# Half of the last block's weights, split into their two parts where they are converted and stored from SyncE

## The chip, the core and the metric

The kernel runs on one core of one Trainium2 chip. The metric is the device time of one execution in microseconds, as the median of three runs; lower is better. A difference under about 0.2%, some 4 us here, can hardly be told from no change.

## The reference

Three layers follow one another, for 2304 tokens of 512 features: a linear attention, a mixture of eight experts in which every token passes through every expert, and a dense block with the activation h - tanh(h). Cut to what matters:

```python
attn = linear_attention(q, k, v, omega)          # 4 x 8 heads x 576 x 64
x = attn.transpose(0, 2, 1, 3).reshape(2304, 512)
P = balanced_softmax(x @ w_gate)                 # 2304 x 8
out = 0
for e in range(8):                               # w1: 8 x 512 x 1024, w2: 8 x 1024 x 512
    out += P[:, e:e + 1] * (maximum(x @ w1[e], 0) @ w2[e])
h = out @ w_in                                   # w_in: 512 x 2048, drawn as doubles
return (h - tanh(h)) @ w_out                     # w_out: 2048 x 512, doubles
```

The weights of the last block are 64-bit numbers in DRAM; everything else is float32.

## The kernel before

Every matrix product is made of three products of rounded parts: a float32 operand is held as a high part, rounded for TensorE, and a low part, the rest. `split` (L107, L110) makes them: ScalarE casts the high part, and GpSimd or VectorE subtracts it from the source. A tile `u` (128 x 2 x 256) holds the two parts of one piece of a first-layer weight, a tile `v` (128 x 2 x 512) those of a second-layer weight; 16 tiles u and 8 tiles v stand in rings.

The tokens are cut into three superblocks of 768. The experts are done for all three, one superblock after another, and then the last block for all three. In the second and third superblock the products of the experts are made by a scheme with seven products for eight; their weights' parts come back from DRAM copies (`u<-st` at L290, `y<-st` at L312), which SyncE loads, in the order of the program, into rings of 16 and 12 pieces. A step of an expert's loop is a "quad", of which a superblock has 32.

The last block goes through its 2048 hidden features in four groups of 512, g = 0 to 3, for each superblock. For a group it needs eight tiles u and four tiles v. The generator `weights()` makes them: jobs of kind "i" load 512 KB of the float32 copy `win32` into a tile `rqi` and split four tiles u from it, with the subtraction on GpSimd; jobs of kind "s" load 256 KB of `wout32` into a tile `rs` and split one tile v, two of a group's four on GpSimd and two on VectorE. This is done again for every superblock, as the two parts don't stay in SBUF. In `shrink` the product `p` (L1481) is turned into h - tanh(h) by ScalarE and VectorE, its high part is cast by ScalarE (L1509), and its low part is made by GpSimd (L1510); `l` (L1521) is the product with `v`.

The float32 copies are made by `convert`, since no engine reads doubles: VectorE takes a piece of 128 x 256 doubles `r` apart in six instructions, with one of ScalarE and one of GpSimd between, and SyncE stores the float32 piece `x` (L1179). There are 64 pieces, 16 for each group. It runs in the background, a step at a time: 27 pieces in the first superblock, where a step follows every third tick, and 37 in the third, where a piece takes eight steps. There a piece's tile `r` is one of a ring of three (tag "rs"), and the load of piece k+3 (L1150) is issued right behind the store of piece k.

All loads and stores named here stand in SyncE's one queue, in the program's order; an entry that waits holds up those behind it. Each also waits for the one issued eight places before it.

Of the kernel before, what the change touches and what calls it, by code (L numbers as in the profile page):

```python
# [10 lines left out]
F32 = mybir.dt.float32  # L11
# [9 lines left out]
def performer_moe_kernel(ctx, tc, q, k, v, omega, wg, w1, w2, win64, wout64, out):  # L21
    nc = tc.nc
# [60 lines left out]


    CW = 256
    cjobs, made, converted = [], {}, [0]

    def to_convert(src, dst, r, c):
        cjobs.append((src[r : r + P, c : c + CW], dst[r : r + P, c : c + CW]))

    for g in range(NGM):
        for f in range(g * GF, (g + 1) * GF, 2):
            for r in range(0, DM, P):
                to_convert(win64, win32, r, f * P)
            made["i", f] = len(cjobs)
        for f in range(g * GF, (g + 1) * GF):
            for c in range(0, DM, CW):
                to_convert(wout64, wout32, f * P, c)
            made["o", f] = len(cjobs)
    NCV = len(cjobs)  # L100

    u1, u2, uw = {}, {}, {}
    spent1, spent2, spentx, spentw = set(), set(), set(), set()
# [80 lines left out]
    def weights():  # L184
# [2 lines left out]
        jobs = []  # L187
        for Q in range(NQ):
            e, q = divmod(Q, NQE)
            jobs.append(("q", Q, lambda e=e, q=q: load_quad(e, q), 0))  # L190
            for f in (2 * q, 2 * q + 1):
                jobs.append(("s", 2 * Q + f % 2, lambda e=e, f=f: load_slab(w2[e][f * P : (f + 1) * P, :]), 0))
        for g in range(NG + 1):
            jobs.append(("c", g, None, 0))
        for s in range(NSB):
            for g in range(NGM):
                for f in range(g * GF, (g + 1) * GF, 2):
                    jobs.append(("i", 0, lambda f=f: load_win(f), NCV if s else made["i", f]))
                for f in range(g * GF, (g + 1) * GF):
                    jobs.append(  # L200
                        (
                            "s",
                            -1,
                            lambda f=f: load_slab(wout32[f * P : (f + 1) * P, :]),
                            NCV if s else made["o", f],
                        )
                    )
        ahead = []

        def slabs(Q):  # L210
# [3 lines left out]
        def fetch():  # L214
            while jobs and len(ahead) < 5:
                k = jobs[0][0]
                if jobs[0][3] > converted[0]:
                    break
                if k == "c":
                    if ahead:  # L220
                        break
                elif sum((x[0] == "s") == (k == "s") for x in ahead) >= (3 if k == "s" else 2):
                    break
                elif k != "s" and not rqfree():
                    break
                k, a, f, _ = jobs.pop(0)
                ahead.append((k, a, f and f()))
# [18 lines left out]
        while ahead or jobs:  # L246
# [75 lines left out]
            elif k == "i":  # L322
                raw, done = raw
                for i in range(4):
                    while not free1(n1):
                        yield 1
                    o = i // 2 * P
                    unit1(n1, raw[:, i % 2 * 2 : i % 2 * 2 + 2, o : o + P], nc.gpsimd)
                    n1 += 1
                    yield None  # L330
                done[0] = True
            else:
                while not free2(n2):
                    yield 1
                k = (n2 - N2) % NV - NU2 if n2 >= N2 else -1
                if k < 0:
                    u = vtile([P, 2, 512], f"v{n2}", lambda n=n2: n in spent2)
                elif k == 0:
# [7 lines left out]
                if a >= 0:  # L346
# [793 lines left out]
    def convert(raws, work, fine):  # L1140
        V = nc.vector
        bits = lambda w: struct.unpack("f", struct.pack("I", w))[0]
        big, small = bits(0x47EFFFFF), bits(0x38100000)

        def ld():
            if not cjobs or halt[0]:
                return None
            src, dst = cjobs.pop(0)
            r = raws(f"r64_{len(cjobs)}")
            nc.sync.dma_start(r, src.bitcast(U32).rearrange("p (n t) -> p n t", t=2))  # L1150
            return r, dst

        nx = [ld(), ld()] if fine else [ld()]
        for _ in range(16 if fine else 1):
            yield
        while nx[0]:
            r, dst = nx.pop(0)
# [8 lines left out]
            yield  # L1166
            V.scalar_tensor_tensor(h, c, 0xC0000000, t, ALU.bitwise_and, ALU.bitwise_or)
            if fine:
                yield
            V.tensor_scalar(t, h, 0xFF800000, None, ALU.bitwise_and)  # L1170
            yield
            V.scalar_tensor_tensor(xf, lo, 2.0**-52, t.bitcast(F32), ALU.mult, ALU.mult)
            yield
            nc.scalar.activation(cf, cf, AF.Abs)
            nc.gpsimd.tensor_tensor(xf, xf, h.bitcast(F32), ALU.add)
            yield
            yield
            V.scalar_tensor_tensor(xf, cf, small, xf, ALU.is_ge, ALU.mult)
            nc.sync.dma_start(dst, xf)  # L1179
            converted[0] += 1  # L1180
            yield


# [457 lines left out]
    for st in stages:  # L1641
# [47 lines left out]
        elif kind == 0:  # L1689
            for Q in range(NQ):  # L1690
                e, g = Q // NQE, (s - 1) * NQ + Q
                if s == 1 and Q == 0:
                    set_banks("ppn", 4, 4)
                    kept.extend(lbank("l2") for _ in range(2))
                if s == 1 and Q == 1:
                    first_turn()
                if s == 2 and Q == 1:
                    halt[0] = False
                    pace[4] = 26
# [112 lines left out]
```

## Time and profile before

| | before |
|---|---|
| median of three runs | 2061.15 us (2060.12 to 2062.38) |
| the profiled execution's own time | 2059.81 us |
| its span, first to last instruction | 2058.0 us |
| TensorE (PE) busy | 2011.1 us, 98% of the span |
| VectorE (DVE) busy | 1562.3 us, 76% |
| ScalarE (ACT) busy | 1420.8 us, 69% |
| GpSimd (POOL) busy | 1471.3 us, 71% |

The profiled execution lies 1.34 us under the median of the runs. PE's busy time is that of pipelined matmuls; what counts is where it is idle, and what ended that idle time.

### The profile page before, as it was taken

Reading aid. Unit: us, or ns where it says so; the run is one execution under the profiler, and the core shown is the slowest. Engines: PE = TensorE matmul, PEld = TensorE weight load, DVE = VectorE, ACT = ScalarE, POOL = GpSimd, SP = SyncE. Lnnn points to the kernel's source line nnn. Section 1 sums busy time; section 2 is a strip of 40 time slices with the busy share of each in tenths; the row PEclk is TensorE's granted clock in tenths of the full one; section 3 lists DMA queues with packets and bytes.
Section 4 is the critical chain, followed back from the end, with each engine's and each line's share of the span. In section 5 each row is a group of like instructions: output and inputs, shape, how many; then the busy total and the mean of one; then the engine's idle time right before and its main releaser. Section 6 shows DMA issues by size and latency. Waiting matters only on the chain.

```text
span 2058.0 us, 37571 instructions
## 1 busy us (share of the span) xinstructions
PE 2011.1 (98%) x11408; PEld 1878.2 (91%) x11408; DVE 1562.3 (76%) x3004; ACT 1420.8 (69%) x3498; POOL 1471.3 (71%) x1855
## 2 busy tenths in 40 slices
PE   8999999999999999999999999999999989999999
PEld 7776888898999899999999999999999878989998
DVE  8885768889886665666666667777775589999997
ACT  7885333443442577777777688788788878888885
POOL 7885877887784588888888767676676675565652
PEclk9999999999999999999999999999999999999999
DMA  6545977798786688999988988988878532131310
GB/s 172 136 140 176 367 273 272 274 334 278 274 277 238 198 279 308 346 329 332 332 311 307 346 284 294 336 287 287 300 271 300 179 116 77 62 127 43 113 47 31
DMA packets 348056, 486.45 MB, mean 236 GB/s; under 512 B 71616, under 2 KB 166736, under 8 KB 347856
## 3 DMA queue, kind: packets, MB, share of 16 engines
q1 hardware_dynamic: 341712, 476.66, 67.6%
q10 hardware_dynamic: 6144, 7.40, 1.1%
q8 instruction: 92, 1.51, 0.3%
q14 instruction: 108, 0.88, 0.1%
HBM read 339.17 MB, written 144.78 MB: 235 GB/s over the span
## 4 chain that ended last, share of the span: by engine, by line
PE 79%; DVE 6%; POOL 6%; ACT 3%; issue 3%; DMA 2%; SPq 0%; ACTq 0%; DVEq 0%; POOLq 0%
PE l L1521 21%; PE Y L1380 18%; PE b L1205 13%; PE e L1205 9%; PE a L1205 8%; PE p L1481 7%; PE X L1380 2%; POOL tmp L616 2%; POOL eq L776 1%; POOL h L1289 1%; DMA y<-st 1%; DVE t L1502 0%; POOL u L110 0%; DVE t L1503 0%; DVE x L110 0%
## 5 line engine op out<-in xcount | busy, mean ns | idle before, releaser
L1380 PE MATMUL Y<-h,y 128*128 128x384 f32 x2394 | 486.3, 336 | 9.5 <-ACT Y L1372 9.0
L1521 PE MATMUL l<-v,h 128*128 128x512 f32 x2016 | 483.6, 393 | 8.9 <-POOL h L1510 3.8
L1521 PEld LDWEIGHTS l<-v,h 128*128 128x128 f32 x2016 | 375.5, 188 | 87.5 <-POOL h L1510 4.7
L1380 PEld LDWEIGHTS Y<-h,y 128*128 128x128 f32 x2394 | 419.9, 188 | 15.4 <-ACT Y L1372 14.5
L1289 POOL TENSOR_TENSOR h<-t,h 128x384 fp32r<-128x384 f32 x223 | 229.9, 1031 | 175.7 <-ACT h L1286 147.6
L1205 PE MATMUL b<-x,u 128*128 128x384 f32 x1728 | 348.5, 336 | 2.2 <-DVE t L1299 1.7
L1396 ACT COPY seven<-Y 128x384 f32<-128x384 f32 x534 | 247.1, 482 | 134.9 <-PE Y L1380 131.7
L1205 PEld LDWEIGHTS b<-x,u 128*128 128x128 f32 x1728 | 304.9, 188 | 8.0 <-DVE t L1299 2.0
L1372 ACT COPY Y<-seven 128x384 f32<-128x384 f32 x558 | 263.0, 488 | 3.8 <-DVE seven L1394 3.8
L1289 POOL TENSOR_TENSOR h<-h,h 128x384 fp32r<-128x384 f32 x192 | 203.6, 1066 | 43.3 <-ACT h L1286 40.1
L1205 PE MATMUL a<-x,u 128*128 128x384 f32 x1152 | 231.6, 335 | 1.6 <-POOL u L110 1.3
L1205 PE MATMUL e<-x,u 128*128 128x384 f32 x1152 | 231.2, 335 | 0.0
L1481 PE MATMUL p<-x,u 128*128 128x384 f32 x1152 | 210.6, 338 | 1.9 <-DVE seven L1394 1.9
L1481 PEld LDWEIGHTS p<-x,u 128*128 128x128 f32 x1152 | 203.8, 189 | 5.8 <-DVE seven L1394 2.2
L1205 PEld LDWEIGHTS a<-x,u 128*128 128x128 f32 x1152 | 202.3, 188 | 3.3 <-POOL u L110 1.7
L1205 PEld LDWEIGHTS e<-x,u 128*128 128x128 f32 x1152 | 202.5, 188 | 0.0
L110 POOL TENSOR_TENSOR v<-rs,v 128x256 fp32r<-128x256 f32 x176 | 144.0, 846 | 63.3 <-ACT v L107 54.9
L1510 POOL TENSOR_TENSOR h<-t,h 128x384 fp32r<-128x384 f32 x94 | 96.3, 1025 | 122.5 <-ACT h L1509 117.7
L1286 ACT CAST h<-t 128x384 fp32r<-128x384 f32 x224 | 115.7, 518 | 35.4 <-POOL t L1342 17.8
L1304 DVE TENSOR_TENSOR t<-b,t 128x384 f32<-128x384 f32 x64 | 35.6, 556 | 123.1 <-PE b L1205 123.1
L1556 DVE SCALAR_TENSOR_TENSOR acc<-l,pt,acc 128x512 f32<-128x512 f32 x144 | 104.7, 744 | 27.6 <-PE l L1521 25.9
L107 ACT CAST u<-s 128x256 fp32r<-128x256 f32 x128 | 49.4, 409 | 105.8 <-POOL u L110 42.0
(346 smaller groups left out, 3817.0 us busy)
## 6 DMA issues: line engine op xcount, KB each, us to landing
u<-st SPq DMA_DIRECT2D x448, 256.0 KB, 5.2
y<-st SPq DMA_DIRECT2D x336, 256.0 KB, 5.0
st<-u SPq DMA_DIRECT2D x224, 256.0 KB, 3.9
rs<-in_moe_w_dram SPq DMA_DIRECT2D x128, 256.0 KB, 4.8
st<-y SPq DMA_DIRECT2D x128, 256.0 KB, 5.7
st<-v SPq DMA_DIRECT2D x96, 256.0 KB, 5.2
rq<-in_moe_w_dram SPq DMA_DIRECT2D x32, 512.0 KB, 4.7
rqi<-win SPq DMA_DIRECT2D x24, 512.0 KB, 4.8
```

Source lines behind the costliest of these rows:

```text
L107: nc.scalar.copy(dst[:, 0], src)
L110: eng.tensor_tensor(dst[:, 1, i : i + w], src[:, i : i + w], dst[:, 0, i : i + w].bitcast(F32), ALU.subtract)
L1205: nc.tensor.matmul(ps[:, :TB], u[:, wi, c], x[:, xi, c], start=(start and m == 0), stop=(stop and m == 5), skip_group_check=True,)
L1286: nc.scalar.copy(H[k][:, 0], src)
L1289: eng.tensor_tensor(H[k][:, 1], src, H[k][:, 0].bitcast(F32), ALU.subtract)
L1372: nc.scalar.copy(cell[0], xacc[i][:, d])
L1380: nc.tensor.matmul(ps, uw[i, g][0][:, wi, d * P : (d + 1) * P], Hs[g][i][:, hi], start=(n == 0 and not cell), stop=(n == 3 * len(gs) - 1), ...
L1396: nc.scalar.copy(xacc[i][:, d], ps)
L1481: nc.tensor.matmul(ps, u1[f + i][:, wi, c], ux[state["x0"] + 2 * t + i][:, xi, c], start=(m == 0), stop=(m == 11))
L1510: nc.gpsimd.tensor_tensor(lo, s, hi.bitcast(F32), ALU.subtract)
L1521: nc.tensor.matmul(ps, hh[f][0][:, hi, t : t + P], u2[n + f][:, wi], start=(f == 0 and i == 0), stop=(f == len(hh) - 1 and i == 2),)
L1556: V.scalar_tensor_tensor(a, ps, p[:, e : e + 1], a, ALU.mult, ALU.add)
```

## The change

The conversion's list is cut in two. The pieces of groups 3 and 2 come first, in the first superblock, as before in float32. The 32 pieces of groups 0 and 1 are put at the head of the list when the third superblock begins. There, once a piece is float32 in `x`, VectorE makes its two parts in the place of its doubles (the tile `r` has room for both): a cast and a subtraction. SyncE stores them to new DRAM tensors `st3` (two stores for a piece of w_in) and `st4` (one for a piece of w_out). The load of piece k+3 is issued behind that store of piece k. In the last block, new jobs "i2" and "v" load the parts of groups 0 and 1 straight into tiles u and v, for each of the three superblocks.

```diff
+    st3 = [dp.tile([P, 2, 2, 2, 2, P], F32, name=f"st3_{i}") for i in range(GF)]
+    st4 = [dp.tile([P, 2, DM], F32, name=f"st4_{i}") for i in range(2 * GF)]
...
+        early = key[1] < 2 * GF
+        job = (key, src[r : r + P, c : c + CW], parts if early else plain[r : r + P, c : c + CW])
+        (later_jobs if early else cjobs).append(job)
...
+            elif k == "i2":
+                for i in range(4):
+                    while not free1(n1):
+                        yield 1
+                    nc.sync.dma_start(tile1(n1).bitcast(F32), st3[a // 2][:, i // 2, i % 2])
+                    n1 += 1
+                    if i % 2:
+                        yield None
...
-                split(u, raw, nc.vector if on_v else nc.gpsimd, 1 if on_v else 2)
+                if k == "v":
+                    nc.sync.dma_start(u.bitcast(F32), st4[a])
+                else:
+                    split(u, raw, nc.vector if on_v else nc.gpsimd, 1 if on_v else 2)
...
+        after = []
+
+        def step():
+            f = after.pop(0) if after else None
+            if f:
+                f()
+
+        def split_up(x, r, dst, key):
+            both = r.rearrange("p n t -> p (n t)").rearrange("p (h n) -> p h n", h=2).bitcast(F32R)
+
+            def low():
+                V.tensor_tensor(both[:, 1], x, both[:, 0].bitcast(F32), ALU.subtract)
+
+            def put():
+                for to, src in dst(both.bitcast(F32)):
+                    nc.sync.dma_start(to, src)
+                left[key] -= 1
+
+            return [None, None, lambda: V.tensor_copy(both[:, 0], x), None, low, None, put]
...
-        nx = [ld(), ld()] if fine else [ld()]
+        nx = [ld(), ld(), ld()] if fine else [ld()]
...
-            nx.append(ld())
+            r, dst, key = nx.pop(0)
+            if not fine:
+                nx.append(ld())
...
             V.scalar_tensor_tensor(xf, cf, small, xf, ALU.is_ge, ALU.mult)
-            nc.sync.dma_start(dst, xf)
+            if callable(dst):
+                after.extend(split_up(xf, r, dst, key))
+            else:
+                nc.sync.dma_start(dst, xf)
+                left[key] -= 1
+            if fine:
+                after.append(lambda: nx.append(ld()))
             converted[0] += 1
+            yield
+            step()
```

One `step()` follows each of a piece's eight yields, so the cast, the subtraction, the store and the next load of a piece fall into the eight steps of the piece after it.

On SyncE (a row is a DMA, with the semaphores that it waits for; DMAHW ones tell of other DMAs), early in the third superblock, at the end of its first piece. Before:

```order
L290 DMA u481_16304<-st1_4_83 128x512 [waits DMAHW6_49]
L1179 DMA wout32_76<-cw27x_16182 128x256 [waits DMAHW7_49,DVE_49]
L1150 DMA r64_33_16327<-in_moe2_w_out_dram 128x512 [waits DMAHW0_49]
L312 DMA y264_16354<-st2_3_114 128x512 [waits DMAHW1_49,PE_49]
L290 DMA u482_16356<-st1_4_83 128x512 [waits DMAHW2_49]
L312 DMA y264_16354<-st2_3_114 128x512 [waits DMAHW3_49]
```

Of the change, there:

```order
L296 DMA u485_16430<-st1_5_84 128x512 [waits DMAHW6_49]
L1176 DMA st3_0_143<-r64_36_15946 128x2x128 [waits DMAHW7_49,DVE_49]
L1176 DMA st3_0_143<-r64_36_15946 128x2x128 [waits DMAHW0_49]
L1186 DMA r64_33_16457<-in_moe2_w_in_dram 128x512 [waits DMAHW7_49,DMAHW1_49,DMAHW0_49]
L318 DMA y268_16513<-st2_4_115 128x512 [waits DMAHW2_49,PE_49]
L296 DMA u486_16515<-st1_5_84 128x512 [waits DMAHW3_49]
```

The load of `r64_33` waited for one earlier DMA, the entry eight places back; now it waits for three, of which two (DMAHW1 and DMAHW0) are the stores right ahead of it, which read the tile that it fills.

On VectorE, in the third superblock, around the piece that follows (`cw29`; `r64` is a tile of doubles, and the rows without cw or r64 are the expert's own). Before:

```order
L1162 TENSOR_SCALAR cw29_16468<-r64_34_16179 128x256
L1165 TENSOR_SCALAR cw29_16468<-cw29_16468 128x256
L1331 TENSOR_TENSOR t1_35_16496<-b7_35_16272,h11_35_16397 128x384
L1332 TENSOR_TENSOR t3_35_16497<-h22_35_16371,b7_35_16272 128x384
L1167 SCALAR_TENSOR_TENSOR cw29_16468<-cw29_16468 128x256
L1170 TENSOR_SCALAR cw29_16468<-cw29_16468 128x256
L1299 TENSOR_TENSOR t1_7_36_16478<-b7_36_16475,t0_7_36_16477 128x384
L1172 SCALAR_TENSOR_TENSOR cw29x_16469<-r64_34_16179,cw29_16468 128x256
```

Of the change, there:

```order
L1199 TENSOR_SCALAR cw29_16480<-r64_34_15950 128x256
L1203 TENSOR_SCALAR cw29_16480<-cw29_16480 128x256
L1385 TENSOR_TENSOR t1_35_16508<-b7_35_16284,h11_35_16408 128x384
L1386 TENSOR_TENSOR t3_35_16509<-h22_35_16381,b7_35_16284 128x384
L1179 CAST r64_35_15948<-cw28x_16339 128x256
L1206 SCALAR_TENSOR_TENSOR cw29_16480<-cw29_16480 128x256
L1210 TENSOR_SCALAR cw29_16480<-cw29_16480 128x256
L1353 TENSOR_TENSOR t1_7_36_16490<-b7_36_16487,t0_7_36_16489 128x384
L1172 TENSOR_TENSOR r64_35_15948<-cw28x_16339,r64_35_15948 128x256
L1213 SCALAR_TENSOR_TENSOR cw29x_16481<-r64_34_15950,cw29_16480 128x256
```

Two instructions have come in, the cast and the subtraction of piece 28 into its `r64` tile, among the first six instructions of piece 29.

On GpSimd, where the last block begins (the low parts `h0_0_0_...` that L1510 makes are waited for by the first `l`). Before, from the second of them to the fourth:

```order
L1510 TENSOR_TENSOR h0_0_0_1_22390<-s0_0_0_1_22308,h0_0_0_1_22390 128x384
L110 TENSOR_TENSOR u686_22397<-rqi_22246,u686_22397 128x256
L110 TENSOR_TENSOR u687_22400<-rqi_22246,u687_22400 128x256
L1510 TENSOR_TENSOR h0_0_0_2_22427<-t3_0_0_0_2_22383,h0_0_0_2_22427 128x384
L110 TENSOR_TENSOR v68_22434<-rs_22269,v68_22434 128x256 x2
L110 TENSOR_TENSOR v69_22444<-rs_22284,v69_22444 128x256 x2
L1510 TENSOR_TENSOR h0_0_0_3_22490<-t3_0_0_0_3_22420,h0_0_0_3_22490 128x384
L110 TENSOR_TENSOR u688_22504<-rqi_22440,u688_22504 128x256
```

Of the change, the first to the fourth (L1510 is L1564 there), with the two sums of the experts' end between them:

```order
L1564 TENSOR_TENSOR h0_0_0_0_22373<-s0_0_0_0_22269,h0_0_0_0_22373 128x384
L1470 TENSOR_TENSOR seven3_9481<-seven3_9481,seven2_9480 128x768
L1470 TENSOR_TENSOR seven5_9483<-seven5_9483,seven1_9479 128x768
L1564 TENSOR_TENSOR h0_0_0_1_22452<-s0_0_0_1_22366,h0_0_0_1_22452 128x384
L1564 TENSOR_TENSOR h0_0_0_2_22485<-t3_0_0_0_2_22445,h0_0_0_2_22485 128x384
L1564 TENSOR_TENSOR h0_0_0_3_22531<-t3_0_0_0_3_22478,h0_0_0_3_22531 128x384
```

The splits of u and v that stood between the low parts are gone; no other row of GpSimd stands between them.

## Rows read from the trace of the kernel before

**Rows 1.** The page, busy time, share and instructions of each engine.

```profile
PE 2011.1 (98%) x11408; PEld 1878.2 (91%) x11408; DVE 1562.3 (76%) x3004; ACT 1420.8 (69%) x3498; POOL 1471.3 (71%) x1855
```

**Rows 2.** Busy time of each engine in three stretches, the clock and the DMA share.

```profile
core 0: us, PE busy (x) PEld busy (x) DVE busy (x) ACT busy (x) POOL busy (x), PEclk, DMA share, GB/s
1196.00:1576.00 380.00, 376.43 (x2155) 372.67 (x2154) 272.37 (x500) 310.08 (x755) 264.08 (x268) 1.00 0.85 296
1626.00:1706.00 80.00, 68.09 (x340) 61.53 (x341) 64.33 (x94) 63.92 (x145) 57.04 (x58) 0.96 0.32 109
1706.00:1822.00 116.00, 115.85 (x587) 105.34 (x586) 110.19 (x171) 97.98 (x217) 71.83 (x76) 1.00 0.31 101
```

**Rows 3.** Waits of PE, 1626 to 1706 us: total, times, longest.

```profile
PE Y L1380 <- ACT Y L1372: 4.4, 4, 1.8
PE l L1521 <- POOL h L1510: 3.8, 2, 3.3
PE l L1521 <- ACT h L1509: 1.9, 2, 1.4
PE p L1481 <- DVE seven L1394: 1.9, 1, 1.9
```

**Rows 4.** Timeline, 1661 to 1674 us: start, length, what, idle time before it.

```profile
1664.45 3.86 POOL L110 TENSOR_TENSOR v<-rs,v 128x256 fp32r<-128x256 f32 x4
...
1669.63 0.79 PE L1521 MATMUL l<-v,h 128*128 128x512 f32 x1 [3.33 <-POOL h L1510]
...
1670.23 3.89 PE L1481 MATMUL p<-x,u 128*128 128x384 f32 x12
```

**Rows 5.** Timeline of PE, 1625 to 1634 us.

```profile
1627.93 2.25 PE L1481 MATMUL p<-x,u 128*128 128x384 f32 x12
```

**Rows 6.** Instructions by group, 1626 to 1706 us: count, busy us, mean ns, idle before.

```profile
L110 POOL TENSOR_TENSOR u<-rqi,u 128x256 fp32r<-128x256 f32 x24 | 21.5, 915 | 3.5 <-ACT u L107 2.8 <-DMA rs<-wout 0.7
...
L110 POOL TENSOR_TENSOR v<-rs,v 128x256 fp32r<-128x256 f32 x9 | 8.1, 919 | 0.6 <-ACT v L107 0.6
...
L107 ACT CAST u<-rqi 128x256 fp32r<-128x256 f32 x22 | 8.0, 404 | 2.1 <-DMA rqi<-win 1.2 <-POOL seven L1416 0.9
```

**Rows 7.** Instructions of DVE by group, 1196 to 1576 us.

```profile
L1162 DVE TENSOR_SCALAR cw<-r 128x256 f32<-128x256 f32 x36 | 23.1, 641 | 0.6
L1167 DVE SCALAR_TENSOR_TENSOR cw<-cw 128x256 uint32<-128x256 uint32 x36 | 18.7, 519 | 0.7
...
L1165 DVE TENSOR_SCALAR cw<-cw 128x256 uint32<-128x256 uint32 x36 | 15.8, 439 | 0.5
...
L1304 DVE TENSOR_TENSOR t<-b,t 128x384 f32<-128x384 f32 x25 | 13.9, 555 | 52.7 <-PE b L1205 52.7
```

**Rows 8.** Waits of PE, 1196 to 1576 us.

```profile
PE Y L1380 <- ACT Y L1372: 3.5, 7, 0.8
```

**Rows 9.** Waits of SP's own queue, 1196 to 1576 us.

```profile
SPq L312 <- PE Y L1380: 62.0, 47, 6.5
...
SPq L1179 <- DVE cw55x L1178: 7.4, 1, 7.4
...
SPq L312 <- PE X L1380: 6.0, 1, 6.0
...
SPq L1179 <- DVE cw60x L1172: 0.2, 1, 0.2
```

**Rows 10.** Line L1162, 1196 to 1576 us: ns min/median/max, first and last start.

```profile
L1162 DVE TENSOR_SCALAR cw<-r x36: 276/464/1104, 1201.3 to 1567.9; 128x256 f32<-128x256 f32 x36
```

**Rows 11.** Line L1179 (stores of converted pieces), 1196 to 1576 us.

```profile
DMA to landing us min/median/max: 1.9/4.7/7.0
```

**Rows 12.** Line L1150 (loads of doubles), 1196 to 1576 us.

```profile
DMA to landing us min/median/max: 3.1/4.8/6.9
```

**Rows 13.** Line L312 (loads of y), 1618 to 1626 us.

```profile
L312 SPq DMA_DIRECT2D y<-st x4: 319/376/433, 1618.4 to 1623.0; - x4
...
DMA to landing us min/median/max: 2.7/2.8/3.0
```

More of the change, by code (lines that the diff above doesn't have):

```diff
@@ L85, in performer_moe_kernel, with to_convert @@
     CW = 256
[L86 to L91, printed above, removed]
-        for f in range(g * GF, (g + 1) * GF, 2):
-            for r in range(0, DM, P):
-                to_convert(win64, win32, r, f * P)
-            made["i", f] = len(cjobs)
+    cjobs, later_jobs, left, converted = [], [], {}, [0]
+    def to_convert(key, src, r, c, plain, parts):
+        left[key] = left.get(key, 0) + 1
+        early = key[1] < 2 * GF
+        job = (key, src[r : r + P, c : c + CW], parts if early else plain[r : r + P, c : c + CW])
+        (later_jobs if early else cjobs).append(job)
+    for g in (3, 2, 0, 1):
+        for f in range(g * GF, (g + 1) * GF, 2):
+            for r in range(NC):
+                parts = lambda x, f=f, r=r: [
+                    (st3[f // 2][:, j, r // 2, :, r % 2], x[:, :, j * P : (j + 1) * P]) for j in range(2)
+                ]
+                to_convert(("i", f), win64, r * P, f * P, win32, parts)
         for f in range(g * GF, (g + 1) * GF):
             for c in range(0, DM, CW):
-                to_convert(wout64, wout32, f * P, c)
-            made["o", f] = len(cjobs)
-    NCV = len(cjobs)
+                parts = lambda x, f=f, c=c: [(st4[f][:, :, c : c + CW], x)]
+                to_convert(("o", f), wout64, f * P, c, wout32, parts)
     u1, u2, uw = {}, {}, {}
@@ L197, in weights @@
                 for f in range(g * GF, (g + 1) * GF, 2):
-                    jobs.append(("i", 0, lambda f=f: load_win(f), NCV if s else made["i", f]))
+                    if f < 2 * GF:
+                        jobs.append(("i2", f, None, ("i", f)))
+                    else:
+                        jobs.append(("i", 0, lambda f=f: load_win(f), ("i", f)))
                 for f in range(g * GF, (g + 1) * GF):
[L200 to L207, printed above, removed]
+                    if f < 2 * GF:
+                        jobs.append(("v", f, None, ("o", f)))
+                    else:
+                        load = lambda f=f: load_slab(wout32[f * P : (f + 1) * P, :])
+                        jobs.append(("s", -1, load, ("o", f)))
         ahead = []
@@ L216, in fetch @@
                 k = jobs[0][0]
-                if jobs[0][3] > converted[0]:
+                if jobs[0][3] and left[jobs[0][3]]:
                     break
@@ L221, in fetch @@
                         break
-                elif sum((x[0] == "s") == (k == "s") for x in ahead) >= (3 if k == "s" else 2):
+                elif k == "s" and sum(x[0] == "s" for x in ahead) >= 3:
                     break
-                elif k != "s" and not rqfree():
+                elif k in "qi" and (sum(x[0] in "qi" for x in ahead) >= 2 or not rqfree()):
                     break
@@ L334, in weights @@
                     yield 1
-                k = (n2 - N2) % NV - NU2 if n2 >= N2 else -1
-                if k < 0:
+                part = (n2 - N2) % NV - NU2 if n2 >= N2 else -1
+                if part < 0:
                     u = vtile([P, 2, 512], f"v{n2}", lambda n=n2: n in spent2)
-                elif k == 0:
+                elif part == 0:
                     u = w2p[1].tile([P, 2, 512], F32R, tag="v", name=f"v{n2}")
@@ L342, in weights @@
                 on_v = n2 >= N2 and n2 % GF > 1
-                split(u, raw, nc.vector if on_v else nc.gpsimd, 1 if on_v else 2)
+                if k == "v":
+                    nc.sync.dma_start(u.bitcast(F32), st4[a])
+                else:
+                    split(u, raw, nc.vector if on_v else nc.gpsimd, 1 if on_v else 2)
                 u2[n2] = u
                 n2 += 1
-                if a >= 0:
+                if k == "s" and a >= 0:
                     st = st2[a // 2]
@@ L1164, in convert @@
                 yield
+                step()
             V.tensor_scalar(t, c, 3, 0x3FFFFFFF, ALU.logical_shift_left, ALU.bitwise_and)
             yield
+            step()
             V.scalar_tensor_tensor(h, c, 0xC0000000, t, ALU.bitwise_and, ALU.bitwise_or)
@@ L1169, in convert @@
                 yield
+                step()
             V.tensor_scalar(t, h, 0xFF800000, None, ALU.bitwise_and)
             yield
+            step()
             V.scalar_tensor_tensor(xf, lo, 2.0**-52, t.bitcast(F32), ALU.mult, ALU.mult)
             yield
+            step()
             nc.scalar.activation(cf, cf, AF.Abs)
@@ L1176, in convert @@
             yield
+            step()
             yield
+            step()
             V.scalar_tensor_tensor(xf, cf, small, xf, ALU.is_ge, ALU.mult)
-            nc.sync.dma_start(dst, xf)
+            if callable(dst):
+                after.extend(split_up(xf, r, dst, key))
+            else:
+                nc.sync.dma_start(dst, xf)
+                left[key] -= 1
+            if fine:
+                after.append(lambda: nx.append(ld()))
             converted[0] += 1
+            yield
+            step()
+        while after:
+            step()
             yield
@@ L1698, in performer_moe_kernel @@
                     halt[0] = False
+                    cjobs[:] = later_jobs + cjobs
                     pace[4] = 26
```

11 lines of the change are left out of this document (5 added, 6 removed).

## The prediction

> **What bounds the kernel now.** I began with the page's line of the engines [rows 1]: TensorE is busy 98% of the span and no other engine above 76%. So work taken from VectorE, ScalarE or GpSimd, or given to them, counts only where TensorE waits for it. The table of stretches [rows 2] says where that is. In the last block's steady part (1706 to 1822 us) TensorE is busy 115.85 of 116 us: splits that are taken out there buy nothing. Between 1626 and 1706 us, where the experts end and the last block begins, it is busy 68.09 of 80 us, and its granted clock is 0.96. In the third superblock, where the change adds work, it idles 3.57 of 380 us. So there is one place to gain, one place to lose, and the rest is covered.
>
> The waits of the first place [rows 3] have four parts that sum to 12.0 us: 4.4 for `Y` on ScalarE, 3.8 for `l` on GpSimd's low part of `h`, 1.9 for `l` on ScalarE's high part, 1.9 for `p` on VectorE's sums of the experts. The timeline [rows 4] shows the worst: `l` waits 3.33 us for GpSimd, which was busy with four subtractions of `v` for 3.86 us ahead of that low part. Behind that wait twelve matmuls of `p` take 3.89 us; the same twelve took 2.25 us a little earlier [rows 5]. That is the lower of the clock's two levels, 1.2 in place of 2.4 GHz, after an idle stretch.
>
> **The change part by part. What it removes.** Groups 0 and 1 are no longer split in the last block. In the first place that takes 24 subtractions of `u` and 9 half tiles of `v` off GpSimd, 21.5 + 8.1 = 29.6 us of its 57.04, and 8.0 us of casts off ScalarE [rows 2, 6]. The order shows the low parts of `h` with no split between them.
>
> The idle time there is 80 − 68.09 = 11.9 us. The clock of 0.96 means that about 4% of 80 us is missing; at half speed that is some 6.4 us spent at the lower level, in which half as much work is done, so about 3.2 us lost. The one row that shows it directly is smaller, 3.89 − 2.25 = 1.64 us for one run of twelve matmuls. I take 1.6. Together 13.5 us, at the most 11.9 + 3.2 = 15.1, can come back. Not all will: of the wait on VectorE's sums (1.9) and of the 3.3 us for ScalarE's `Y` and `h` that don't come from the splits alone, I leave half, some 3 us. **Gain 10.5 us, bounds 7.3** (the waits for `h` alone and the clock: 3.8 + 1.9 + 1.6) **and 15.1.**
>
> What takes the splits' place are loads. The first of them stand in SyncE's queue right behind the last loads of `y`, which were issued until 1623.0 us at 0.4 us apiece and landed in 2.8 us, at most 3.0 [rows 13]. So the first tile `u` lands near 1623.0 + 0.8 + 3.0 = 1626.8 us, and `p` began at 1627.93 [rows 5]: cost 0, with TensorE's last expert matmuls as cover. With a landing of 4.8 us, as loads of that size take in the busy third superblock [rows 12], it would be 0.7 us late. After that a group needs 12 tiles for each superblock, at a DMA share of 0.31 to 0.32 before [rows 2]; the loads of `win32` that they replace carried half the bytes. Cost 0.
>
> **What it adds** lies in the third superblock: 32 pieces with a cast and a subtraction of 128x256 each on VectorE. Near kin there: 0.44 us (L1165) for the cast, 0.52 us (L1167) for the subtraction [rows 7], so 32 × 0.96 = 31 us; from the slower kin, 0.64 (L1162) and, if the subtraction runs at twice the fastest, 1.0, it is 32 × 1.64 = 52 us. VectorE is busy 272.37 of 380 us there, 107.6 us are free, and of these 52.7 are spent waiting for TensorE's `b` in one group alone [rows 7]. The sum is covered. But the `t` and `b` behind a late instruction come up to a microsecond later, and TensorE's own slack toward VectorE isn't in any row; today none of its 3.5 us of waits there is for VectorE [rows 8]. Bounds 0 and 32 × 0.2 = 6 us (a fifth of each piece's added time uncovered); I take 3.
>
> Then the stores. A piece goes out as two parts, twice the bytes and one or two DMAs in place of one. DMA share is 0.85 at 296 GB/s [rows 2]. 32 × 128 KB more are 4.2 MB, 14 us at that rate, against 0.15 × 380 = 57 us that the engines stand free. Covered, with later landings.
>
> Then SyncE's queue, the dearest unknown. The load of piece k+3 used to follow the store of a different tile and waited for nothing. Now it fills the tile that the stores right ahead of it read, so it waits until they have landed: 1.9 / 4.7 / 7.0 us (least, median, most) [rows 11]. In 23 of the 32 places nothing stands between store and load in the new order, in 9 some 5 to 9 other entries do. Taken for all 32, 4.7 − 0.6 of issue = 4.1 us each, 131 us in which no `y` and no `u` behind it is issued. Against it stand the queue's own waits of today: 62.0 us for `Y` to free a tile, 6.0 for `X`, 46 in the 21 rows for VectorE's pieces (7.4 the longest, 0.2 the last, both printed) [rows 9], together 114 us. The 23 tight places alone are 94 us, under 114. So most of the new wait takes the place of waiting that is there anyway, since a `y` that is issued late was waiting for its tile. A single block of 4 to 7 us is about the length of the longest wait for `Y` now, 6.5.
>
> Last the doubles themselves. A piece takes (1567.9 − 1201.3) / 35 = 10.47 us [rows 10], 1.31 us a step. From the store's step to the first use of the tile that is then loaded there are ten steps, 13.1 us. Less the store's landing 4.7, the load's 4.8 [rows 11, 12] and its issue 0.3, 3.3 us are left in the median; at the slowest, 13.1 − 7.0 − 6.9 = −0.8, before any lateness of SyncE. VectorE then stalls with an expert's work behind it. I put 2 us for a few such stalls; 0 to 15 for the range (a stall of 0.8 at half of the pieces is 13).
>
> **Sum.** Loss 3 + 2 = 5, gain 10.5: −5.5 us. Of the profiled execution, 2059.81 − 5.5 = 2054.3; the median lies 1.34 above it, so **2055.6 us**. The first superblock converts 27 pieces as before and the last block's steady part is full anyway: 0.
>
> **A rule that speaks against it.** The Trainium skill, "DMA: Bandwidth & Descriptors", section "Anatomy of one DMA", says that a DMA has about 2 us of fixed cost that is mostly the confirmation of the write, and that a semaphore wait happens on the issuing sequencer before dispatch; the least landing here, 1.9 us, agrees [rows 11]. By it 32 × 2 = 64 us of queue would be empty, against the 57 us for which the DMA engines are free: 7 us over, and the sum would be about +1.
>
> **The rivals.** *All of the gain and no loss.* Speaks for it: VectorE has 107.6 us free and TensorE waits for nobody but ScalarE there. Time −9 to −15, near 2049.5 by the median (−11.7). Against: the waits on ScalarE and VectorE in the first place aren't all due to splits. 0.14.
>
> *Given back in the third superblock.* VectorE's stalls and its two more instructions reach TensorE for 6 to 15 us. Place: the `t` and `b` of an expert's step that stand behind a late `r64`. Time within 4 us of before, 2057 to 2065. For it: a margin of 3.3 us that is gone when SyncE comes late by as much. 0.28.
>
> *The queue blocks, slower.* If every one of the 32 loads holds SyncE for 4.1 us, 131 − 114 = 17 us are over, `y` comes late and TensorE waits for DMA: +17 − 10.5 = +6.5, 2067.6. It decides from the point where the blocks pass 114 us, 3.6 us for each of 32. For it: a median landing that is above that. Against: nine of the places have other entries between. 0.20.
>
> *The forecast*, −4.2 to −9: 0.38.
>
> That the change doesn't do what it says is no rival here: the order shows the splits gone.
>
> **How the numbers follow.** 0.2% is 4.1 us, about what can be told here from no change. Faster by more is the forecast and the full gain, 0.38 + 0.14 = 0.52; within it 0.28; slower 0.20. The likeliest is 2055.6. The range leaves out the better part of the full gain's far end and of the slower rival's: 2048.5 to 2066. The forecast's own is 2052 to 2057.
>
> **What would show it.** Right: in the stretch that answers to 1626 to 1706 us some 3 us of idle and a clock of 1.00, with no wait for GpSimd's `h`; in the third superblock VectorE busier by about 31 us, TensorE idle by 6 to 9 us in all, SyncE's waits at the load of doubles near 4 us, 20 and more of them, and its waits for `Y` shorter by as much. Wrong: TensorE waiting for the DMA of `y` (the third rival), VectorE waiting for `r64` with TensorE behind it by over 10 us (the second), or the first `p` waiting for the DMA of `u`.

## The result: slower by 1.5%, and the profile after

The changed kernel takes 2091.81 us (median of four runs, 2088.66 to 2092.59) against 2061.13 us: ratio 1.0146, 95% interval 1.0128 to 1.0163, 30.7 us slower. The forecast was 2055.6 us and its range ended at 2066. The profiled execution took 2088.66 us, 3.2 less than that median.

The span of the profiled execution grew by 28.9 us, from 2058.0 to 2086.9. Where it went is read from one line, the first `p` of the last block (it stood at 1627.93 us [rows 5]). Changed kernel, the line of `p`: ns least/median/most, first and last start:

```profile
L1535 PE MATMUL p<-x,u x1152: 332/334/522, 1663.1 to 2066.6; 128*128 128x384 f32 x192
```

Up to that matmul 35.2 us are lost; from there to the end 35.2 − 28.9 = 6.3 us are won. Both signs of the forecast are there, but the loss is seven times what it was put at.

Changed kernel, the stretches that answer to [rows 2]: the third superblock, the experts' end (35 us later now), the steady part.

```profile
core 0: us, PE busy (x) PEld busy (x) DVE busy (x) ACT busy (x) POOL busy (x), PEclk, DMA share, GB/s
1196.00:1576.00 380.00, 352.72 (x1958) 345.06 (x1957) 278.28 (x522) 284.11 (x688) 243.35 (x244) 0.98 0.82 277
1661.00:1741.00 80.00, 72.80 (x365) 65.53 (x364) 62.89 (x98) 59.41 (x131) 39.77 (x38) 0.98 0.52 176
1741.00:1857.00 116.00, 115.82 (x586) 105.27 (x586) 109.00 (x171) 92.12 (x199) 54.30 (x55) 1.00 0.38 131
```

In the third superblock TensorE now idles 27.3 us in 380 where it idled 3.6, and the clock is 0.98. At the experts' end idle time fell from 11.9 to 7.2 us and the clock rose from 0.96 to 0.98, some 1.6 us more: 4.7 + 1.6 = 6.3, about the gain. The steady part stands as it stood.

Changed kernel, waits of PE, 1661 to 1741 us (they answer to [rows 3]):

```profile
PE Y L1434 <- ACT Y L1426: 2.3, 3, 1.5
PE p L1535 <- DMA u<-st: 1.6, 2, 1.3
PE l L1575 <- ACT h L1563: 1.3, 1, 1.3
PE l L1575 <- DVE acc L1600: 0.9, 1, 0.9
PE p L1535 <- DVE seven L1448: 0.8, 1, 0.8
PE l L1575 <- DMA rs<-wout: 0.3, 1, 0.3
```

The wait for GpSimd's `h` is gone, as forecast; new is 1.6 us for the first tiles `u`, which now come by a load.

Changed kernel, waits of PE, 1190 to 1660 us; before, the third superblock had only the one for `Y` [rows 8]:

```profile
PE b L1259 <- DVE t L1358: 13.4, 5, 5.3
PE Y L1434 <- ACT Y L1426: 10.5, 14, 2.2
PE b L1259 <- DVE t L1353: 4.9, 2, 4.3
```

Why VectorE is late is the next view: its own waits, 1190 to 1660 us. L1199 is a piece's first instruction, the one that reads `r64`.

```profile
DVE cw L1199 <- DMA r<-in_moe_w_out_dram: 39.6, 11, 10.1
...
DVE cw L1199 <- DMA r<-in_moe_w_in_dram: 21.8, 9, 5.8
```

61.4 us in 20 waits, where the forecast put 2 us for such stalls. The queue that brings `r64` shows why. Changed kernel, waits of SP's queue, 1196 to 1576 us (before: [rows 9]); L1186 is the load of doubles, L1176 the stores ahead of it:

```profile
SPq L1186 <- DMA st<-r: 125.3, 32, 6.4
...
SPq L318 <- PE Y L1434: 7.0, 17, 1.5
SPq L318 <- PE X L1434: 6.5, 1, 6.5
...
SPq L1176 <- DVE cw L1203: 1.0, 3, 0.5
...
SPq L1176 <- DVE b L1336: 0.2, 1, 0.2
```

Of the 32 loads that follow a store of parts, 29 wait for it (three of them twice, which makes 32 waits): the 23 with nothing between store and load 4.9 us each, 113.4 in all; six of the nine that have other entries between (four, or eight) 11.9 us in all; three not at all. Against these 125.3 us the queue's other waits shrank: for `Y` 62.0 became 7.0, for VectorE 46 us became 7.9 (13 rows, the first and the last are shown).

How much of the new wait took the place of old is read over the same piece of the program, since 380 us of the changed kernel hold less of it. From 1190 us to the first `p` (437.9 us before, 473.1 now) the rows of SP's waits sum to 214 us before and 231 now: 125.3 are new, and 108 were given up, 43 of waits for TensorE, 40 for VectorE, 24 for other DMAs. SyncE's issues there took 213 us before and 232 now. Together 17 + 19 = 36 us, about the 35 by which the last block comes late. Waits and issues fill the queue's time whatever it does, so this sum shows where SyncE's time went and no cause; the experiments do that.

One such place. Changed kernel, timelines of SP, VectorE and PE, 1308 to 1325 us: start, length, engine, what, idle time before:

```profile
1312.18 0.59 SPq L1176 DMA_DIRECT2D st<-r  x1
1318.39 0.34 SPq L1186 DMA_DIRECT2D r<-in_moe_w_out_dram  x1
1318.82 0.38 SPq L318 DMA_DIRECT2D y<-st  x1
...
1310.83 0.54 DVE L1353 TENSOR_TENSOR t<-b,t 128x384 f32<-128x384 f32 x1
1321.51 0.29 DVE L1199 TENSOR_SCALAR cw<-r 128x256 f32<-128x256 f32 x1 [10.14 <-DMA r<-in_moe_w_out_dram]
...
1322.58 0.55 DVE L1358 TENSOR_TENSOR t<-b,t 128x384 f32<-128x384 f32 x1
...
1313.60 1.20 PE L1259 MATMUL b<-x,u 128*128 128x384 f32 x6
...
1323.19 2.29 PE L1259 MATMUL b<-x,u 128*128 128x384 f32 x6 [5.27 <-DVE t L1358]
```

SyncE issues the store, then nothing for 5.6 us (1312.77 to 1318.39), then the load; the doubles land, VectorE goes on after 10.14 us of idling and makes the expert's `t`, and TensorE, 5.27 us idle, can make the next `b`, at the lower of its two clock levels: six matmuls in 2.29 us, 1.20 us ten microseconds before.

### The profile page after: what moved, and what is told of

It is laid out like the page before. It is cut to its first block, busy times and chain, and to the rows that moved or that the text cites. A ratio compares the mean times of both kernels' runs of the same rounds, so it can differ in the third digit from the quotient of the medians.

```text
span 2086.9 us, 37530 instructions
## 1 busy us (share of the span) xinstructions
PE 2021.9 (97%) x11408; PEld 1885.1 (90%) x11408; DVE 1574.3 (75%) x3056; ACT 1395.7 (67%) x3426; POOL 1410.0 (68%) x1783
## 4 chain that ended last, share of the span: by engine, by line
PE 69%; DMA 10%; DVE 9%; POOL 5%; issue 3%; ACT 2%; SPq 1%; ACTq 0%; DVEq 0%; POOLq 0%
PE l L1575 20%; PE Y L1434 13%; PE b L1259 11%; PE p L1535 8%; PE e L1259 7%; PE a L1259 7%; DMA st<-r 3%; PE X L1434 2%; DMA u<-st 2%; POOL tmp L633 2%; DMA y<-st 1%; POOL eq L793 1%; DMA r<-in_moe_w_out_dram 1%; DMA r<-in_moe_w_in_dram 1%; DMA st<-y 1%
## 5 line engine op out<-in xcount | busy, mean ns | idle before, releaser
L1434 PE MATMUL Y<-h,y 128*128 128x384 f32 x2394 | 491.5, 338 | 14.1 <-ACT Y L1426 13.6
L1259 PEld LDWEIGHTS b<-x,u 128*128 128x128 f32 x1728 | 306.2, 189 | 28.3 <-DVE t L1358 15.1
L1564 POOL TENSOR_TENSOR h<-t,h 128x384 fp32r<-128x384 f32 x94 | 95.9, 1020 | 187.9 <-ACT h L1563 185.7
L116 POOL TENSOR_TENSOR v<-rs,v 128x256 fp32r<-128x256 f32 x152 | 121.3, 827 | 53.6 <-ACT v L113 41.1
L116 POOL TENSOR_TENSOR u<-s,u 128x256 fp32r<-128x256 f32 x128 | 97.4, 778 | 22.5 <-ACT u L113 21.8
```

The costliest lines, as they stand in the source:

```text
L116: eng.tensor_tensor(dst[:, 1, i : i + w], src[:, i : i + w], dst[:, 0, i : i + w].bitcast(F32), ALU.subtract)
L1259: nc.tensor.matmul(ps[:, :TB], u[:, wi, c], x[:, xi, c], start=(start and m == 0), stop=(stop and m == 5), skip_group_check=True,)
L1434: nc.tensor.matmul(ps, uw[i, g][0][:, wi, d * P : (d + 1) * P], Hs[g][i][:, hi], start=(n == 0 and not cell), stop=(n == 3 * len(gs) - 1), ...
L1564: nc.gpsimd.tensor_tensor(lo, s, hi.bitcast(F32), ALU.subtract)
```

## The experiments

Three theories were set against each other. Theory 1: the late tile, as in the timeline above, is the cause by itself. Theory 2: the blocked queue is, since whatever stands behind the load is late, be it `r64`, `u` or `y`. Theory 3: it is the 64 more instructions on VectorE. The steps at which a piece is split, stored and followed by a load are counted from its end, here and in the expectations: the first is the piece's own last, the second the next piece's first. Medians, each beside runs of the kernel before on the same chip; "first p" and "rest" are the shift of the first `p` against 1627.93 us and of what follows it (shift of the span less that), from one profile each. A profile can lie off its median: late's by −2.7 us, late2's by +2.1, ring4_wait's by +3.3, dve_only's by −1.2, ring4_free's by −2.5:

| run | us | ratio (95%) | first p | rest |
|---|---|---|---|---|
| ring4 | 2059.37 | 0.9993 (0.9984 to 1.0003) | +6.8 | −7.3 |
| early | 2080.83 | 1.0097 (1.0082 to 1.0112) | +29.0 | −8.1 |
| late | 2066.22 | 1.0027 (1.0018 to 1.0037) | +3.3 | +0.4 |
| ring4_wait | 2086.87 | 1.0122 (1.0108 to 1.0137) | +36.0 | −5.9 |
| late2 | 2077.97 | 1.0084 (1.0070 to 1.0097) | +19.1 | +1.1 |
| ring4_pool | 2062.17 | 1.0008 (0.9999 to 1.0017) | +9.6 | −8.0 |
| ring4_g0 | 2061.45 | 1.0004 (0.9995 to 1.0013) | +3.4 | −2.1 |
| wait_only | 2092.19 | 1.0146 (1.0131 to 1.0162) | +32.0 | +0.6 |
| gap | 2065.25 | 1.0024 (1.0015 to 1.0033) | +13.0 | −7.8 |
| dve_only | 2067.46 | 1.0035 (1.0021 to 1.0049) | +5.4 | +1.1 |
| ring4_early | 2065.81 | 1.0025 (1.0015 to 1.0035) | +14.5 | −8.5 |
| ring4_free | 2056.47 | 0.9984 (0.9975 to 0.9992) | +2.6 | −8.4 |

**ring4**: a fourth tile, so that the load no longer fills the tile that is just being stored.

```diff
+    turns = [0]
+
+    def fourth(n):
+        turns[0] += 1
+        if turns[0] % 4:
+            return rawp.tile([P, CW, 2], U32, tag="rs", name=n, bufs=3)
+        return cxp[0].tile([P, CW, 2], U32, tag="r", name=n, bufs=1)
...
-                            lambda n: rawp.tile([P, CW, 2], U32, tag="rs", name=n, bufs=3),
+                            lambda n: fourth(n),
```

> The changed kernel with a fourth tile for the doubles, so that the load of piece k+3 fills the tile of piece k-1, whose store was issued a piece (some 11 us) earlier. Theory 1 (late tile: VectorE stands before an r64 that has not landed, 61 us in all, with the expert's t behind it): the waits for r64 nearly vanish and the third superblock loses under 5 us; 2055 to 2059 us, faster than before. Theory 2 (blocked queue: SyncE's 125 us of waits for its own stores delay u and y): those waits vanish too, the same time; this run tells both from theory 3 alone. Theory 3 (the 32 casts and subtractions on VectorE, 22 us, reach TensorE): nothing changes, 2085 to 2092 us.

28 of the 35 us are gone, with the same instructions, stores and bytes; the time is that of the kernel before (the interval holds 1), not faster as theories 1 and 2 had it. This ring4 profile has, 1196 to 1576 us, for SP's queue:

```profile
SPq L318 <- PE Y L1441: 77.6, 51, 5.2
```

The queue runs ahead again and waits for TensorE. Theories 1 and 2 stand; 3 can at most explain the 6.8 us that are left.

**early** (three tiles; the split and the store sooner):

```diff
-            return [None, None, lambda: V.tensor_copy(both[:, 0], x), None, low, None, put]
+            return [lambda: V.tensor_copy(both[:, 0], x), low, put]
```

> The changed kernel with the cast, the subtraction, the store and the load in the first four steps of the next piece in place of steps 3, 5, 7 and 8: tile and queue entries are the same, only some four steps (5 us) earlier. Theory 1: VectorE's waits for r64 fall from 61 to 5 to 20 us, TensorE's loss with them; 2058 to 2070 us. Theory 2: SyncE still waits 32 times some 4 us at the load; 2085 to 2092. Theory 3: the same instructions, 2085 to 2092.

The time lies between the two ranges: VectorE's waits for `r64` fell from 61 to 35 us, and 29 of the 35 us of loss remained. SyncE's waits at the load stayed, 1190 to 1660 us:

```profile
SPq L1186 <- DMA st<-r: 115.1, 27, 6.6
```

Part of what VectorE no longer waits is waited for elsewhere: TensorE now has 3.4 us for the DMA of `y`.

**late** and **late2**: the kernel before, its load moved later; no store is waited for. Late2 issues it behind the second step of the piece ahead of its own; the lines are late's.

```diff
-        nx = [ld(), ld()] if fine else [ld()]
+        nx = [ld(), ld(), ld()] if fine else [ld()]
+        first = True
...
             r, dst = nx.pop(0)
-            nx.append(ld())
+            if not fine:
+                nx.append(ld())
...
             converted[0] += 1
             yield
+            if fine and not first:
+                nx.append(ld())
+            first = False
```

> The kernel before with one thing changed: the load of piece k+3 is issued eight steps later, at the place it has in the changed kernel, and waits for no store of that tile. Lead in the median: eight steps or 10.5 us less SyncE's lag of some 7 us and a landing of 3.3 us, about 0. Theory 1: VectorE waits for r64 at about half of the pieces, some 20 to 40 us, and TensorE loses 5 to 20; 2066 to 2081 us. Theory 2: SyncE waits for no store, so nothing changes; 2060 to 2063.

> The kernel before with only the load of the doubles moved, two steps later still than in the run before (six steps, 7.9 us, ahead of its use), with no wait for a store. Theory 1: VectorE waits for r64 some 50 to 100 us in all and TensorE loses 20 to 45 us; 2081 to 2106 us. Theory 2: SyncE waits no longer than before, so 2061 to 2068 us.

Late cost 5.6 us by the medians, at the lower edge of theory 1's range; its tiles were rarely late (13 us of waits in 5, not the 20 to 40 expected). Late2, waits of VectorE, 1190 to 1660 us:

```profile
DVE cw L1164 <- DMA r<-in_moe_w_in_dram: 16.3, 4, 7.5
DVE cw L1164 <- DMA r<-in_moe_w_out_dram: 13.6, 5, 6.0
```

With 30 us of such waits, fewer than I expected, and no store waited for, 17 us are lost by the medians. The queue isn't blocked: it waits 99.2 us for TensorE's `Y` (1190 to 1660 us). So a late tile does cost TensorE by itself; theory 1 isn't wrong as a mechanism.

**ring4_wait**: the fourth tile for a fourth piece in flight; the wait is back, the tile has time. `fourth` is ring4's.

```diff
-        nx = [ld(), ld(), ld()] if fine else [ld()]
+        nx = [ld(), ld(), ld(), ld()] if fine else [ld()]
```

> The changed kernel with the fourth tile of doubles, used for a fourth piece in flight: the load behind the store of piece k is that of piece k+4, into the tile that the store reads. SyncE so waits for its own stores as in the changed kernel, but a tile has a whole piece (some 10 us) more until its use. Theory 1 (late tile): VectorE hardly waits for r64; 2058 to 2065 us. Theory 2 (blocked queue): SyncE's waits at that load stay at 100 to 130 us in all, u and y come late; 2080 to 2092 us.

Nearly the whole loss is back: by the medians 25.9 us, 30.7 in the changed kernel. Waits of PE, 1190 to 1710 us, in ring4_wait:

```profile
PE Y L1441 <- DMA y<-st: 13.1, 7, 2.6
PE Y L1441 <- ACT Y L1433: 6.4, 9, 1.9
PE b L1266 <- DMA u<-st: 5.2, 3, 1.8
```

VectorE waits only 6.5 us for `r64` here; TensorE waits for `y` and `u` instead, which had no such rows before. Theory 1 as the sole cause falls: with the late tile taken away, the queue's loss shows in the tiles of the experts.

**wait_only**: the kernel before, in which a piece's last instruction writes into `r64` and the store reads it there. Instructions, bytes and entries of the queue are the same.

```diff
-            V.scalar_tensor_tensor(xf, cf, small, xf, ALU.is_ge, ALU.mult)
-            nc.sync.dma_start(dst, xf)
+            y = r.rearrange("p n t -> p (n t)")[:, :CW].bitcast(F32) if fine else xf
+            V.scalar_tensor_tensor(y, cf, small, xf, ALU.is_ge, ALU.mult)
+            nc.sync.dma_start(dst, y)
```

> The kernel before with one thing changed: in the third superblock the last of a piece's six instructions writes the float32 piece into the tile of its doubles in place of x, and the store reads it there. Instructions, bytes, entries of the queue and their places are the same; only the load of piece k+3 now waits until the store right ahead of it has landed, 37 times some 4 us. The tiles have a piece more of time than in the changed kernel. Theory 2 (the blocked queue alone costs TensorE): SyncE's waits at that load 120 to 160 us in all, 2081 to 2100 us. Theory 1 (only a late tile costs): 2060 to 2066 us.

This one dependency, at 37 pieces, costs as much as the whole change does on balance (31.5 and 30.7 us by the medians). Wait_only, waits of SP's queue, 1190 to 1660 us:

```profile
SPq L1150 <- DMA wout<-r: 77.6, 17, 6.7
SPq L1150 <- DMA win<-r: 59.9, 15, 6.2
SPq L312 <- PE Y L1381: 33.8, 35, 6.5
```

and waits of its PE, 1190 to 1665 us:

```profile
PE Y L1381 <- DMA y<-st: 15.5, 9, 4.3
```

137.5 us of waits; of the 32.0 us of shift 2.9 stood already ahead of the second superblock in this execution (its first `X` at 700.6 us, 697.7 before), so 29 us for 37 pieces; by the piece that is some 25 for the 32 of the change, an estimate. VectorE waits only 7.9 us for `r64` here; the tile that TensorE waits for longest is `y`.

**gap**: the changed kernel with its three tiles; the cast, the subtraction and the store in the first three steps, the load in the eighth as it was.

```diff
-            return [None, None, lambda: V.tensor_copy(both[:, 0], x), None, low, None, put]
+            return [lambda: V.tensor_copy(both[:, 0], x), low, put, None, None, None, None]
```

> The changed kernel with three tiles, as it is, but the cast, the subtraction and the store in the first three steps of the next piece and the load where it was, in the eighth: five steps (some 6.5 us) lie between a store and the load behind it. Theory 2: the store has landed when the load's turn comes, SyncE's waits there fall from 125 to under 40 us, and what is left is the 7 us gain against the 7 us that the kernel with the fourth tile lost and 3 to 6 for late tiles: 2060 to 2068 us. Theory 1: the load is issued at the same place of the program, so VectorE's waits for r64 and the time hardly change: 2080 to 2092 us.

Only steps have changed place, and 22 of the 35 us are gone; gap's queue, 1190 to 1660 us:

```profile
SPq L318 <- PE Y L1434: 79.2, 56, 6.5
SPq L1186 <- DMA st<-r: 38.0, 19, 5.1
```

VectorE's waits for `r64` fell to 6.4 us though the load stands where it stood: they had been the queue's lateness. That is what theory 2 had forecast, with its range of 2060 to 2068 us.

**dve_only**: the kernel before with the casts and subtractions, into a tile that nobody reads.

```diff
+            both = cxp[0].tile([P, 2, CW], F32R, tag="d", name=f"d{converted[0]}", bufs=1)
...
+            return [None, None, lambda: V.tensor_copy(both[:, 0], x), None, low]
...
+            if fine and converted[0] < 59:
+                after.extend(split_up(xf))
```

> The kernel before with 32 casts and 32 subtractions more on VectorE in the third superblock, at the steps of the changed kernel, into a tile that nobody reads; stores and loads as before. If VectorE's added work is what is left of the loss with the fourth tile (7 us): 2066 to 2069 us. If it is hidden and the rest comes from the 48 longer stores: 2060 to 2063 us.

As much as ring4 still lost: +5.4 us in the profile, 6.8 by the medians. Dve_only, waits of PE, 1196 to 1576 us:

```profile
PE Y L1408 <- ACT Y L1400: 8.2, 13, 1.2
```

Theory 3 holds for this remainder: the one wait of TensorE there, 3.5 us before [rows 8], more than doubled, though VectorE has 90 us to spare there (289.61 of 380 us busy). The run that was to leave the two instructions out of the changed kernel (**nosplit**) gave no time, so theory 3 is answered from this side only.

**ring4_pool**: the subtraction on GpSimd (`V.tensor_tensor` of `low` became `nc.gpsimd.tensor_tensor`).

> The kernel with the fourth tile (load of k+3 into the tile of k-1), the 32 subtractions on GpSimd in place of VectorE. With the fourth tile the time was 2059.4: 7 us gained in the last block, 7 us still lost in the third superblock, where TensorE waits 11 us for ScalarE's Y. If VectorE's added 22 us (14 of them subtractions) make that remaining loss: 2053 to 2056 us. If it is the stores' traffic or SyncE: 2058 to 2061.

Not better. SyncE then waited 27.6 us for GpSimd at the stores, so the run took something away and added something, and doesn't tell more.

**ring4_g0**: the fourth tile, group 0 alone in parts.

```diff
-        early = key[1] < 2 * GF
+        early = key[1] < GF
...
-                    if f < 2 * GF:
+                    if f < GF:
...
```

> The kernel with the fourth tile, only group 0 (16 pieces) stored in parts, group 1 float32 as groups 2 and 3. The remaining loss in the third superblock should halve (7 to 3 or 4 us) whatever it is made of. If the gain in the last block comes from group 0 alone, it stays at 7: 2055 to 2058 us. If the splits of group 1, which GpSimd makes ahead during group 0, come back between the experts' end and the first l, it falls to 0 to 3: 2059 to 2063 us.

Loss and gain both shrink, +3.4 and −2.1: `l` waits 4.7 us for GpSimd's `h` again, as group 1's splits are made in that stretch. Both groups are needed for the gain.

**ring4_early** and **ring4_free**: the fourth tile, with the two instructions in steps 1 and 2 (and the store and the load in steps 3 and 4), or in steps 6 and 7, where the piece being converted has none on VectorE (store and load where ring4 has them). The lines are ring4_free's.

```diff
-            return [None, None, lambda: V.tensor_copy(both[:, 0], x), None, low, None, put]
+            return [None] * 5 + [lambda: V.tensor_copy(both[:, 0], x), lambda: (low(), put())]
```

> The kernel with the fourth tile, with the cast, the subtraction, the store and the load in the first four steps of the next piece in place of steps 3, 5, 7 and 8. The two late tiles (8 us of VectorE's waits) should go; if the rest of the loss is where VectorE's two instructions fall, it changes too. 2055 to 2059 us if it helps, 2060 to 2064 if not.

> The kernel with the fourth tile, with the cast and the subtraction moved to the sixth and the seventh step of the next piece, the two behind which that piece has no VectorE instruction of its own (ScalarE and GpSimd work on it there); the store with the subtraction, the load in the eighth step. Steps 1 and 2 gave 2065.8 us, steps 3 and 5 gave 2059.4. If what is left of the loss (7 us) is VectorE's instructions following one another between two waits of ScalarE for it: 2052 to 2057 us, faster than before by over 0.2%. If only their number counts: 2058 to 2061.

Steps 1 and 2 lose 14.5 us (2065.81 us, outside both ranges that I had named), steps 3 and 5 lose 6.8, steps 6 and 7 lose 2.6 in their profiles, with the same two instructions. The first of these differences is clear of the noise. Ring4_early and gap, which share steps 1 to 3, agree (2065.8 and 2065.3 us) with four tiles and with three; their waits of PE, 1196 to 1576 us, are one row each, ring4_early's and gap's:

```profile
PE Y L1441 <- ACT Y L1433: 12.4, 14, 2.1
...
PE Y L1434 <- ACT Y L1426: 12.0, 14, 2.1
```

TensorE waits for no DMA there, which speaks for the instructions' place; that the store's place, which both share too, has no part in it isn't shown. The second difference, to ring4_free, is not clear of the noise: its interval overlaps ring4's, and its profile lies 2.5 us under its median, so some 5 us are lost by the medians. Ring4_free beats the kernel before, 2056.47 against 2059.92 us, 0.16% faster (0.08 to 0.25): inside the 2052 to 2057 us expected, short of the 0.2%. In ring4_free the third superblock and the experts' end read:

```profile
1196.00:1576.00 380.00, 373.90 (x2134) 369.11 (x2134) 298.27 (x562) 307.12 (x749) 264.73 (x264) 1.00 0.90 306
1632.00:1712.00 80.00, 74.81 (x383) 67.78 (x384) 65.57 (x101) 61.44 (x133) 40.25 (x37) 1.00 0.52 178
```

## Why the prediction was wrong

**The place and the signs of both parts** were right: a gain at the experts' end, a loss in the third superblock, little elsewhere. Their balance was not.

**The gain** was mis-sized: forecast 10.5 (7.3 to 15.1), measured 6.3, and 5.9 to 8.5 in the runs that keep both groups' loads. GpSimd's wait went, and half of the missing clock came back, the 1.6 us that I took. But 7.2 us of idle stayed where I left 3: of ScalarE's waits (4.4 + 1.9 = 6.3 before; the forecast took 3.3 of them without a row for it) 3.6 stayed, of VectorE's 1.9 there are 1.7, and 1.6 are new for the DMA of `u`, which I had put at 0.

**The queue: the step that failed** is that the wait of the load for the stores ahead of it stands at nothing in the sum, because "most of the new wait takes the place of waiting that is there anyway". Most of it did, 108 of 125.3 us, and yet it was not free: wait_only, which adds this wait and nothing else, loses 29 us, some 25 for the 32 pieces of the change, and ring4 and gap, which take it away, win back 28 and 22 of the 35. Two terms were off besides. The 23 tight places waited 113.4 us, not 94, which is all of the 114 that I held against them; that the total, 125.3, is near the 131 for all 32 is in part luck, as three of the other nine didn't wait at all. And the issues had no place in the sum: 48 stores at a median of 0.53 us, where before 37 took 0.32 each, make some 14 of the 19 us more.

The third rival, at 0.20, had the right root, the blocked queue, and its price of +17 was some 8 short of the 25. Its sign, TensorE waiting for the DMA of `y`, doesn't show in the changed kernel: there the block reaches TensorE by the path of the second rival, 61.4 us of VectorE's waits for `r64` and 18.3 us of TensorE's behind its `t`. The sign of the third shows where `r64` has time, in ring4_wait and wait_only.

The Trainium skill, "DMA: Bandwidth & Descriptors", section "Anatomy of one DMA", was the warning: a semaphore wait sits on the issuing sequencer. The trace agrees, with 5.6 us of an empty queue in the timeline above. Its fixed cost of about 2 us, which the section gives for DMAs that GpSimd issues, is less than half of the least landing of these stores, 4.3 us. The forecast's sum by it set the queue's empty time against the time for which the DMA engines are free; no run shows that the one is paid from the other.

**The late tile** failed in the same step. I gave it 13.1 us from store's step to use, less two landings, as if SyncE issued the store when its step came. In the changed kernel the store is issued 7.2 us (median of 32) after the subtraction is done, where the program has two steps, 2.6 us, between them. The landings were not far off. Changed kernel, stores (L1176), then loads (L1186), 1196 to 1576 us, against 4.7 and 4.8 [rows 11, 12]:

```profile
DMA to landing us min/median/max: 4.3/5.5/7.5
...
DMA to landing us min/median/max: 2.5/3.1/6.6
```

Ring4_wait and gap show that the late tile was one face of the late queue, late2 that it costs by itself when it comes.

**VectorE's instructions** were put at 3 us (0 to 6); dve_only measured 6.8 (4 to 10 by its interval). That there is no wait of TensorE for VectorE in a profile was no proof of slack: in dve_only, too, TensorE's row is for ScalarE's `Y`.

**What makes up the 35 us**: wait_only's 25 and dve_only's 5.4 make 30. The other 5 (the longer stores and their issue, DMA traffic, or the effects adding up to more than each alone) weren't separated and stay open. Where the queue isn't blocked, stores and traffic cost little: ring4 has all of them and loses 6.8 us, 1.4 more than dve_only, which is within the noise.

## What to carry to other kernels

A DMA that waits for another DMA's landing, in a queue that all loads share, holds up everything behind it for that time: put work between the two or give the load another tile, which won back 22 and 28 of the 35 us here. Don't count an in-order queue's waits as spare one for one: 125 us of new wait, 108 of them in place of old ones, still cost some 25. Ask what stands behind each block, and add the issue time of what is new. Where a filler instruction stands in an engine's order may matter as much as its length: the same 64 lost 6.8 us at steps 3 and 5 and 14.5 at steps 1 and 2, though there with the store moved too.

## What the runs showed of the hardware

The casts of 128x256 took 0.28 us at best on VectorE and up to 1.11 us in the third superblock, the subtraction 0.41 to 1.24 us: the same instruction varies by a factor of three or four, and no view here shows why. No instruction in any of the traces takes 64-bit operands: the halves of `r64` are read as f32 and uint32. After idle stretches the granted clock fell to the lower level here too (2.29 us for six matmuls after 5.27 us of idling, 1.20 before): 0.98 over 380 us of the third superblock, in which 2% are 7.6 us, a fifth of the loss.
